# The last 96 columns of w1 ride with the third block of wqkv, and a table fixes the order of the work

## The chip, the cores and the metric

One Trainium2 chip, one core. The metric is the time of one execution on the device, in microseconds (us). TensorE is called PE, VectorE DVE, ScalarE ACT, GpSimd POOL; SyncE (SP) issues every DMA.

## The reference

The input x has 2048 tokens of 512 features. Two branches start from it and meet at the end:

```python
# A: attention, 32 heads of 16 features; each token sees itself and the
# 7 tokens at distances 2, 4, ..., 14 before it
qkv    = x @ wqkv                               # x has been normalised, 512 -> 3 x 512
logits = q . k[pos - 2*w] / 4     (w = 0..7)
o      = softmax(logits) . v[pos - 2*w]
a      = o @ wo
# B: channel mixing, hidden width F = 1376
b      = gelu(layernorm(...) @ w1 + b1) @ w2 + b2
out    = x + a * silu(b)
```

Both branches are fed with normalised rows of x, so that one transposed copy of the normalised tokens serves `x @ wqkv` and `x @ w1` alike.

## The kernel before, in words

**Accuracy.** Each fp32 factor of a product is split in two fp16 parts, a high and a low one, and a product is three matmuls: high by high, low by high, high by low. With a contraction over 512 = 4 x 128 features, that makes 12 matmuls for one output tile. Before a weight is split it is scaled by a power of two found from its sum of squares: ACT squares and accumulates (L421), PE adds up over the partitions (L435), DVE makes the factor (L439 to L459; `hsc` for w1 and the hidden layer, `zsc` for w2, `qsc` for wqkv). Then ACT writes the high part (L482 for w1 and w2, L536 for wqkv) and DVE the low part (L486, L543).

**Tokens.** The even and the odd tokens form two classes c, since all distances are even. A class has 8 token tiles of 128 tokens. `yT` holds their normalised and transposed high and low parts, in four tiles of 512 tokens.

**Attention.** It runs in 8 units, (class c, block hb of 128 features), hb = 0 to 3. In a unit, for each of 8 token tiles, 12 matmuls at L746 hold a piece of yT as the weights and stream 384 columns of `wq` (128 each of q, k and v) past it. ACT (L763) or DVE (L759) brings the 128x384 result into the tile `U`, of which there are two, used in turn. DMAs copy the rows that a token needs from other partitions (the halo, L771, with L776 and L777 for the corner by way of `misc`). DVE then makes the products of q and k (four of 128x2048 at L805), their sums (L808), the softmax (L822 to L837) and the products with v (four, L863); POOL and DVE add these up (L858, L873, L883). ACT and DVE split the result (L846, L848), and a DMA transposes it into `oT` (L851).

**MLP.** It runs in 4 chunks of 512 tokens by 11 blocks f of the hidden width; ten blocks have 128 columns, the last, f = 10, has FL = 96. `mlp1` (L1016) holds 128 (or 96) columns of w1 as the weights and streams 512 tokens of yT, 12 matmuls, into one of 3 PSUM banks `ps`. ACT applies gelu (L1033) and writes the high part (L1036), DVE the low part (L1038), which is the last reader of the bank; `h` has three buffers. `mlp2` (L1052) follows two blocks later: 4 token tiles by 3 matmuls of 512 columns, into 4 banks `z`. For f = 10 the hidden parts stand in a tile `hlast` of their own, whose row 96 holds a one that multiplies the bias b2, which stands as row 96 of w2's last block. The results of class 0 and 1 wait in DRAM (`gd`) until `wo` (L929 for class 0, L961 for class 1) closes the kernel, with a multiplication and an addition per tile on DVE (L993, L1000).

**Banks.** The L746 results use the same 3 banks `ps` and one more, `pl`.

**The order.** All work is first recorded as operations with engine, estimated cost, reads, writes and priority. `Plan.issue` then takes them one by one: at each step it looks at all operations whose inputs are there, takes the engine that can go earliest by its own cost estimates and, on that engine, the operation with the best priority; the DMAs on SP are ordered in the same way. So the program order on every engine comes out of estimates and not out of the text. Ring buffers (`R_ps`, `R_prod`, `R_f`, `R_h` and so on) are given out during this walk, the slot that came free first.

**At the start** the weights pass through buffers that later hold something else: w1's four pieces are loaded into `oT`, one `o` and one `h` buffer, w2 into the class 1 halves of yT and three `f` buffers, and the later blocks of wqkv follow into the same halves of yT when w2 has been split.

Of the kernel before, what the change touches and what calls it, by code (L numbers as in the profile page):

```python
# [18 lines left out]
P = 128  # L19
# [6 lines left out]
NHB = 4  # L26
# [12 lines left out]
LAG = 2  # L39

# [28 lines left out]
BEFORE_W1 = (0, 1, 4, 5)  # L69

# [26 lines left out]
class Plan:  # L97
# [89 lines left out]
    def place(self, o, t):  # L187

        if o.eng == "sp":
            if not o.nbytes:  # L190
                return t
            self.free["sp"] = t + o.issue
            self.dma = max(self.dma, t + o.issue + 0.3)
            self.dma += o.nbytes / (o.rate if self.dma > SLOW else 265e3)
# [12 lines left out]
        if o.port:  # L207
            self.portfree = end
        return end + LAT[o.eng]
# [12 lines left out]
    def issue(self):  # L222
# [104 lines left out]
def tile_mixer(ctx, tc, a_x, a_xt, a_wqkv, a_wo, b_w1, b_b1, b_w2, out):  # L327
# [34 lines left out]
    ident = sb.tile([P, P], F32, name="ident")  # L362
    make_identity(nc, ident)
    fours = sb.tile([P, 2 * P], BF16, name="fours")
    nc.vector.memset(fours, 4.0)
    mean1 = sb.tile([P, P], F32, name="mean1")
# [9 lines left out]
    wq = sb.tile([P, NHB, 2, KT, 384], F16, name="wq")  # L376
    w1 = sb.tile([P, 2, KT * F], F16, name="w1")
# [6 lines left out]
    b1T = sb.tile([P, NF], F32, name="b1T")  # L384
    hlast = sb.tile([P, 2, 512], F16, name="hlast")
# [81 lines left out]
    def low_pool(n, lo, get, s, hi, **k):  # L467
# [4 lines left out]
        pool(0.45 + n * 3.9e-3, fn, **k)  # L472
# [53 lines left out]
    def prep_q(hb):  # L526
# [3 lines left out]
        for k in range(0, KT, st):  # L530
            n = st * 384
            dst = [wq[:, hb, t, k:k + st].rearrange("p k e -> p (k e)") for t in range(2)]
            src = lambda k=k, n=n: stq[hb]()[:, k * 384:k * 384 + n]
# [117 lines left out]
    def y0(i):  # L651
# [12 lines left out]
        elif Y_ENG[i] == "pool":  # L664
            pool(1.25, lambda: nc.gpsimd.tensor_scalar(x(), x(), mv0[:, q, 0:1], rb0[:, q:q + 1], op0=ALU.subtract,
# [54 lines left out]

    def qkv(c, hb, u):
# [13 lines left out]
        raw = pl.users([("xc", j) for j in FP]) if u == 1 else set()  # L735
        csk = {i: (cs, g) for g in parts for i in g} if u == 0 else {i: cs for i in range(NI)}
        for n, i in enumerate((IORD0, IORD1)[u] if u < 2 else IORD):
# [5 lines left out]
            def mm(n0=0, n1=12, y=y, o=o, b=b):  # L743
                for n in range(n0, n1):
                    (s, t), k = ((0, 0), (1, 0), (0, 1))[n // KT], n % KT
                    nc.tensor.matmul(b.t[:, 0:384], y[:, s, k, o:o + P], wq[:, hb, t, k],  # L746
# [5 lines left out]
            for n0, n1 in zip([0] + ends, ends):  # L752
                pe(n1 - n0, 384, lambda mm=mm, n0=n0, n1=n1: mm(n0, n1), [("yh" if n1 <= 4 else "y", c, i)] +
# [8 lines left out]
            else:  # L762
                act(384, lambda i=i, b=b: nc.scalar.activation(  # L763
                    U3[:, i:i + 31:15, :], b.t[:, 0:384].rearrange("p (t e) -> p t e", t=3),
                    AF.Identity, scale=cs.t[:, cp(i):cp(i) + 1]), **ev)

# [241 lines left out]
    def mlp1(ch, f):  # L1008
        M = P if f < NF - 1 else FL
# [15 lines left out]
        if f < NF - 1:  # L1025
            h = R_h.new()
            hi, lo = (lambda: h.t[:, 0]), (lambda: h.t[:, 1])
        else:
            h = ("hlast",)
            hi, lo = (lambda: hlast[:, 0]), (lambda: hlast[:, 1])  # L1030
        hk = (h, 0) if f < NF - 1 else ("hlast", 0)
# [9 lines left out]
        hq[f] = (hi, lo, M if f < NF - 1 else M + 1, h, hk)  # L1041

    def mlp2(ch, f):
        hi, lo, K, h, hk = hq.pop(f)
        for t in range(4):
# [8 lines left out]
            pe(3, 512, mm, [h, hk, w2key[f]] + ([("hrow",)] if f == NF - 1 else []), [zt[t]])  # L1054
# [23 lines left out]
    def mlp(n):  # L1078
        for _ in range(n):
# [4 lines left out]
            if p < len(steps):  # L1084
                with prio(PR_M + p * 10):
                    mlp1(*steps[p])
# [18 lines left out]
    def zero_halo(b):  # L1105
# [7 lines left out]
          lambda: f32v(s1h.t, 1)[:, 0, 0:W1C[4] - W1C[3]]]  # L1113
# [4 lines left out]
    def load(kind, i, last=()):  # L1118
# [6 lines left out]
        elif kind == "w":  # L1125
            dma(P * 4 * (W1C[i + 1] - W1C[i]), lambda: nc.sync.dma_start(s1[i](), b_w1[:, W1C[i]:W1C[i + 1]]), [], s1k[i],
# [4 lines left out]
        elif kind == "b":  # L1131
            dma(P * 44, lambda: nc.sync.dma_start(b1T, b_b1), [], [("b1T",)], rate=20e3)
# [34 lines left out]
    for n in range(WAKE):  # L1167
        b = R_z[0].new()
        pl.add("pe", 0.2, lambda b=b: nc.tensor.matmul(b.t[:, 0:2 * P], fours[:, 0:P], fours, start=True,
# [11 lines left out]
    for n in range(4):  # L1181
        with prio(PS1):
            sumsq(lambda n=n: cw1.t[:, n:n + 1], (cw1, n), s1[n], s1k[n],
                  lambda n=n: w1f[0][:, W1C[n]:W1C[n + 1]], ("w1h", n), W1C[n + 1] - W1C[n])
# [9 lines left out]
    sumsq(lambda: col2.t[:, 0:1], (col2, 0), b1T, ("b1T",), lambda: junk, ("junk",))  # L1194
# [12 lines left out]
    for m, (f0, f1) in enumerate(W1P):  # L1207
        n = min(f0 // 4, 2) if f0 < 10 else 3
        c0, c1 = 512 * f0, min(512 * f1, KT * F)
        with prio(PW1 if m < W1FIRST else PR_H + 1 + (10 * f0 - 25) * 1e-6):  # L1210
            split(w1f[0][:, c0:c1], w1f[1][:, c0:c1], lambda n=n, c0=c0, c1=c1: s1[n]()[:, c0 - W1C[n]:c1 - W1C[n]], hsc[:, 0:1],
                  s1k[n] + [("hsc0",)] + [("w1h", j) for j in range(4) if W1C[j] < c1 and W1C[j + 1] > c0], ("w1", m),
                  W1ENG[m], n=c1 - c0, low=W1LO[m])
    pool(0.1, lambda: nc.gpsimd.memset(hlast[FL:FL + 1, 1], 0.0), [], [("hrow1",)])
    pool(0.6, lambda: nc.gpsimd.memset(hlast[FL:FL + 1, 0], 1.0), [], [("hrow0",)])
    pool(2.0, lambda: nc.gpsimd.tensor_scalar(hlast[FL:FL + 1, 0], hlast[FL:FL + 1, 0],
                                              hsc[FL:FL + 1, 2:3], None, op0=ALU.mult),
         [("hsc2",), ("hrow0",), ("hrow1",)], [("hrow",)])
# [148 lines left out]
```

## Time and profile before

| | |
|---|---|
| time, median of 3 runs | 414.59 us (414.57 to 415.31) |
| the profiled execution | 415.18 us |
| its span, first to last instruction | 413.4 us |
| granted TensorE clock in the span | 0.999 |
| PE, DVE, ACT, POOL busy | 98%, 92%, 54%, 29% |
| mean DMA traffic | 112 GB/s |

The difference between the execution's own time and its span, 1.8 us, lies around the instructions. Of the views used below, the groups of instructions give for each line the count, the total busy time in us and the mean ns of one, and behind the second bar the idle time before them with what ended it; the chain of waits gives the chain of work that ended last, in order of time, with the start, the length, the engine and the line of each step; a timeline gives the same for one engine, with consecutive instructions of one kind put together.

### The profile page before, as it was taken

The page shows a single profiled execution, that of the slowest core. Times are in us where ns is not written, and L with a number is a line of the kernel's source. Part 1 is how long each engine was busy: PE and PEld are TensorE (multiplying, and loading weights), DVE is VectorE, ACT ScalarE, POOL GpSimd, SP SyncE. Part 2 cuts the span into 40 slices and gives each one's busy share as a digit, 9 for nine tenths or more (in the row PEclk, how much of TensorE's full clock was granted, in tenths as well). Part 3 has the DMA queues.
Part 4 walks back from the last instruction along what each step waited for, and adds up shares of the span by engine and source line. Part 5 has one row for each costly group of instructions (what it writes and reads, how often), then busy time and mean ns, then how long its engine had stood idle before and what let it go on. Part 6 is the DMA issues. An engine that isn't in the chain of part 4 may idle for free.

```text
span 413.4 us, 5554 instructions
## 1 busy us (share of the span) xinstructions
PE 405.9 (98%) x2083; PEld 206.6 (50%) x2083; DVE 379.5 (92%) x379; ACT 222.1 (54%) x353; POOL 120.3 (29%) x131
## 2 busy tenths in 40 slices
PE   8799999999999999999999999999999999999996
PEld 5555544445654455445544554455455544444443
DVE  4996989998999999989998999999999998999954
ACT  4699899994549655843384252225212393263500
POOL 3834002004380425042504330434033404520021
PEclk9999999999999999999999999999999999999999
DMA  8958717030045137720172034223604244007133
GB/s 281 397 112 258 235 61 230 0 128 1 1 142 152 28 93 183 149 46 2 48 221 75 0 102 116 68 86 88 205 7 122 88 111 145 0 18 238 23 102 131
DMA packets 47211, 46.41 MB, mean 112 GB/s; under 512 B 31785, under 2 KB 32225, under 8 KB 46673
## 3 DMA queue, kind: packets, MB, share of 16 engines
q1 hardware_dynamic: 47184, 46.06, 37.6%
q8 instruction: 16, 0.26, 0.3%
q14 instruction: 11, 0.08, 0.1%
HBM read 24.06 MB, written 7.34 MB: 76 GB/s over the span
## 4 chain that ended last, share of the span: by engine, by line
PE 92%; ACT 3%; issue 1%; DVE 1%; POOL 1%; ACTq 0%
PE z L1052 28%; PE ps L1016 28%; PE ps L746 25%; PE ps L929 5%; PE ps L961 2%; PE z L961 2%; PE pl L746 1%; ACT w L421 1%; PE pl L961 1%; ACT f L673 1%; ACT yT L687 0%; ACT wq L536 0%; POOL wq L471 0%; POOL rb L635 0%; ACT prod L661 0%
## 5 line engine op out<-in xcount | busy, mean ns | idle before, releaser
L1016 PE MATMUL ps<-yT,w 128*128 128x512 f16 (+1 forms) x528 | 120.4, 379 | 0.0
L746 PE MATMUL ps<-wq,yT 128*128 128x384 f16 x708 | 117.0, 326 | 0.2 <-DVE U L759 0.2
L1052 PE MATMUL z<-w,h 128*128 128x512 f16 x480 | 110.4, 379 | 0.0
L746 PEld LDWEIGHTS <-yT 128*128 128x128 f16 x744 | 72.5, 98 | 49.2 <-issue 1.0
L1016 PEld LDWEIGHTS <-w 128*128 128x128 f16 (+1 forms) x528 | 52.8, 100 | 61.0
L805 DVE TENSOR_TENSOR prod<-U 128x2048 f32<-128x2048 f32 x32 | 73.2, 2286 | 2.2 <-POOL prod L883 0.7
L1052 PEld LDWEIGHTS <-h 128*128 128x128 f16 x480 | 46.6, 98 | 55.5 <-issue 0.3
L808 DVE TENSOR_REDUCE L<-prod 128x128 f32<-128x2048 f32 x32 | 73.0, 2281 | 0.4
L1033 ACT ACTIVATE ps<-ps,b1T,hsc 128x512 f32<-128x512 f32 (+1 forms) x44 | 32.9, 748 | 73.4 <-PE ps L1016 72.2
L863 DVE TENSOR_TENSOR prod<-pl,U 128x2048 f32<-128x2048 f32 x28 | 63.2, 2283 | 4.2 <-POOL prod L873 4.1
L763 ACT ACTIVATE U<-ps,cs 128x384 f32<-128x384 f32 x54 | 31.2, 580 | 65.2 <-PE ps L746 65.2
L873 POOL TENSOR_TENSOR prod<-prod,prod 128x2048 f32<-128x2048 f32 x7 | 31.7, 4531 | 113.8 <-DVE prod L863 99.6
L883 POOL TENSOR_TENSOR prod<-prod 128x1024 f32<-128x1024 f32 x14 | 32.9, 2349 | 0.0
L882 POOL COPY gate<-prod 1x1 f32<-1x1 f32 x21 | 5.5, 264 | 91.0 <-DVE prod L805 82.2
L1038 DVE SCALAR_TENSOR_TENSOR h<-ps,hsc,h 128x512 f16<-128x512 f32 x40 | 29.6, 741 | 1.7 <-ACT h L1036 1.4
L1036 ACT ACTIVATE h<-ps,hsc 128x512 f16<-128x512 f32 x40 | 27.3, 684 | 1.3 <-PE z L1052 0.4
L929 PE MATMUL ps<-wo,oT 128*128 128x512 f16 x96 | 21.7, 379 | 0.0
L858 DVE TENSOR_TENSOR prod<-prod,prod 128x2048 f32<-128x2048 f32 x9 | 20.5, 2282 | 0.0
L1033 ACT ACT_TABLE_LOAD x10 | 12.8, 1283 | 8.6 <-PE ps L1016 8.5
L883 POOL TENSOR_TENSOR prod<-prod,prod 128x1024 f32<-128x1024 f32 x7 | 16.4, 2347 | 0.0
L961 PEld LDWEIGHTS <-oT 128*128 128x128 f16 x108 | 10.6, 98 | 10.4
L929 PEld LDWEIGHTS <-oT 128*128 128x128 f16 x96 | 9.4, 98 | 11.2
(179 smaller groups left out, 377.8 us busy)
## 6 DMA issues: line engine op xcount, KB each, us to landing
f<-in_A_x_dram SPq DMA_DIRECT2D x31, 256.0 KB, 3.5
U<-U SPq DMA_DIRECT2D x16, 392.0 KB, 4.0
gd<-f SPq DMA_DIRECT2D x12, 256.0 KB, 3.4
prod<-in_A_x_dram SPq DMA_DIRECT2D x8, 256.0 KB, 6.9
oT<-in_B_w_dram SPq DMA_DIRECT2D x2, 1024.0 KB
yT<-in_B_w_dram SPq DMA_DIRECT2D x2, 1024.0 KB, 7.9
f<-gd SPq DMA_DIRECT2D x8, 256.0 KB, 2.7
out_dram<-f SPq DMA_DIRECT2D x8, 256.0 KB, 2.8
```

The source lines that it names most:

```text
L746: nc.tensor.matmul(b.t[:, 0:384], y[:, s, k, o:o + P], wq[:, hb, t, k], start=(n == 0), stop=(n == 11))
L763: act(384, lambda i=i, b=b: nc.scalar.activation(U3[:, i:i + 31:15, :], b.t[:, 0:384].rearrange("p (t e) -> p t e", t=3), AF.Identity, sca ...
L805: dve(2048, lambda p2=p2, g=g: nc.vector.tensor_tensor(p2(), q, slots(Ut, KH, 2 * g), op=ALU.mult), qk + [("kh", ub, 0), ("kh", ub, 1), (" ...
L808: dve(2048, lambda pr=pr, g=g: nc.vector.tensor_reduce(L3()[:, 2 * g:2 * g + 2], pr.t.rearrange("p (r f d) -> p r f d", r=2, d=DH), AX.X, ...
L863: dve(2048, lambda: nc.vector.tensor_tensor(pr.t.rearrange("p (r f d) -> p r f d", r=2, d=DH), A3()[:, 2 * g:2 * g + 2].rearrange("p r (f ...
L873: pool(4.75, lambda: nc.gpsimd.tensor_tensor(acc.t, acc.t, p1.t, op=ALU.add), [acc, p1], [acc])
L883: nc.gpsimd.tensor_tensor(x.t[:, 0:1024], x.t[:, 0:1024], y(), op=ALU.add)
L929: nc.tensor.matmul(b.t, oT[:, hb, i // 4, s, i % 4], wo[:, t, hb], start=(hb == 0 and n == 0), stop=(hb == last and n == 2))
L961: nc.tensor.matmul(b.t[:, cols], oT[:, hb, i // 4, s, i % 4], wo[:, t, hb, cols], start=(start and hb == 0 and n == 0), stop=(stop and hb ...
L1016: nc.tensor.matmul(b.t[0:M], w1[:, s, f * 512 + k * M:f * 512 + (k + 1) * M], yT[ch][:, t, k], start=(n == 0), stop=(n == 11))
L1033: act(512, lambda: nc.scalar.activation(b.t[0:M], b.t[0:M], AF.Gelu_apprx_tanh, bias=b1T[0:M, f:f + 1], scale=hsc[0:M, 1:2]), [b, ("b1T",) ...
L1052: nc.tensor.matmul(z.t, hl[s][0:K, t * P:(t + 1) * P], w2[0:K, w, f], start=(f == 0 and n == 0), stop=(f == NF - 1 and n == 2))
```

## The change

**The last 96 columns of w1** are put beside those of block hb = 2 of wqkv: the tile `wq2` is 480 columns wide, and `wl` names its last 96. In the two units with hb = 2 (u = 2 and u = 6) each L746 matmul (L848 in the changed kernel) streams 480 columns and not 384. The first 384 outputs go to `U` as before; ACT brings the other 96 into `hpt` (new, L870), with w1's scale in the same instruction. Here the hidden units lie along the columns and the tokens on the partitions, the other way round than in `mlp1`. So a new function `last_block`, called once per chunk, adds b1 as a row (POOL), applies gelu (ACT), writes the high (ACT) and the low part (DVE), each 128x384 for four token tiles, and a DMA transposes them into `hlt`, which `mlp2` reads for f = 10. The row of ones is set by POOL before the transpose. `mlp1` is no longer made for f = 10, and the three POOL instructions that prepared `hlast` are gone. b1 is loaded with a copy of its last 96 values in every partition, 54.8 KB in place of 5.5. The matmuls of hb = 2 now wait for the last piece of w1 as well.

**The order** no longer comes from the walk: a table ORDER of 1258 operation numbers gives it, and the slot of a ring is the one that came free first in that order. A few cost estimates are changed too, which have no say where the table rules. The constants ident and mean1 move into a tile `first`, which later serves as one of the `hpt`, and the 24 small matmuls without a use that keep PE occupied at the start (L1169, now L1279) read it; in the new order of PE 7 of these 24 stand behind the first L1125 (`mlp1`), where before all stood ahead of the first up-projection.

```diff
+HLAST = 2
+ORDER = (
+    0, 1, 2, 3, 4, 5, 6, 7, 8, 9, 10, 11, 19, 109, 117, 125, 114, 121, 130, 128, 108, 20, 123, 126, 129, 21, 33,
...
+)
@@ Plan.issue
-        order = []
+        order, fixed = [], [self.ops[n] for n in reversed(ORDER)]
...
+            if fixed:
+                o = fixed.pop()
+                t = max([self.earliest(o)] + [min(b.ring.free) for b in o.bufs if b.slot is None])
+                assert not o.npred and t < float("inf")
+                best = (t, o)
-            for e, cand in engs.items():
+            for e, cand in engs.items() if best is None else ():
...
-                    b.ring.free[b.slot] = b.end
+                    b.ring.free[b.slot] = len(order) if ORDER else b.end
@@ tiles
-    wq = sb.tile([P, NHB, 2, KT, 384], F16, name="wq")
-    w1 = sb.tile([P, 2, KT * F], F16, name="w1")
+    wq = [sb.tile([P, 2, KT, 384 + FL * (hb == HLAST)], F16, name=f"wq{hb}") for hb in range(NHB)]
+    w1 = sb.tile([P, 2, W1C[3]], F16, name="w1")
+    wl = wq[HLAST][:, :, :, 384:384 + FL]
...
-    hlast = sb.tile([P, 2, 512], F16, name="hlast")
+    hl0 = sb.tile([P, 512], F32, name="hl0")
+    hpt = [hl0[:, 0:512], first[:, 0:512]]
+    hlt = [h.bitcast(F16).rearrange("p (a t) -> p a t", a=2) for h in hpt]
@@ new
+    def last_block(ch):
+        n = 4 * FL
+        h16 = R_f.new()
...
+        def pads():
+            nc.gpsimd.memset(v()[:, :, :, FL:P], 0.0)
+            nc.gpsimd.tensor_scalar(v()[:, 0, :, FL], halves[:, 8:12], hsc[:, 2:3], 2.0, op0=ALU.mult, op1=ALU.mult)
...
+            pool(1.0, lambda: nc.gpsimd.tensor_tensor(x3(), x3(), row, op=ALU.add), xk + [("b1T",)], xk)
+            act(n, lambda: nc.scalar.activation(x, x, AF.Gelu_apprx_tanh), xk, xk,
+                aps=1, table="gelu")
+            act(n, lambda: nc.scalar.activation(v()[:, 0, :, 0:FL], x3(), AF.Identity, scale=hsc[:, 2:3]),
+                xk + [("hsc2",)], [(h16, 0)])
+            dve(n, lambda: nc.vector.scalar_tensor_tensor(v()[:, 1, :, 0:FL], x3(), hsc[:, 2:3], v()[:, 0, :, 0:FL],
+                                                          op0=ALU.mult, op1=ALU.subtract),
...
+            dma(P * 2048, lambda: nc.sync.dma_start_transpose(dst, h16.t.bitcast(F16)), [(h16, k) for k in range(3)],
@@ qkv
-                    nc.tensor.matmul(b.t[:, 0:384], y[:, s, k, o:o + P], wq[:, hb, t, k],
+                    nc.tensor.matmul(b.t[:, 0:wide], y[:, s, k, o:o + P], wq[hb][:, t, k],
...
+                   ([("w1", len(W1P) - 1)] if hb == HLAST else []) +
...
+            if hb == HLAST:
+                act(FL, lambda i=i, b=b: nc.scalar.activation(
+                    hpt[i // 4][:, (i % 4) * FL:(i % 4 + 1) * FL], b.t[:, 384:384 + FL], AF.Identity, scale=hsc[:, 1:2]),
+                    [b, ("hsc",)], [("hp", i // 4, i % 4)], prio=PEV, after=pl.users([("hp", i // 4, i % 4), ("hl", i // 4)]))
+        for j in range(2 if hb == HLAST else 0):
+            last_block(2 * c + j)
@@ mlp
-            if p < len(steps):
+            if p < len(steps) and steps[p][1] < NF - 1:
```

Three places of the new order matter below; in these rows a number behind a name tells buffers of one ring apart, and it is not the same in the two kernels.

**ACT, splitting w1** (`w_79` before, `w_81` after), from the factor `hsc` to the last high part of w1. Before, its rows stand thus, with two small rows on w2's last block and a table load between them:

```order
L482 ACTIVATE w_79<-oT,hsc 128x512
L482 ACTIVATE w_79<-oT,hsc 128x1024
L763 ACTIVATE U_87<-ps_140,cs_114 128x3x128
L482 ACTIVATE w_79<-oT,hsc 128x1024
L763 ACTIVATE U_86<-pl_142,cs_113 128x3x128
L1262 ACT_TABLE_LOAD
L1262 ACTIVATE warm<-halves 1x1
L482 ACTIVATE w_79<-oT,hsc 128x1024
L763 ACTIVATE U_87<-ps_139,cs_114 128x3x128
L1232 ACTIVATE w_80,s_121<-f_96 97x512
L482 ACTIVATE w_79<-o_105,hsc 128x1024
L482 ACTIVATE w_79<-h_106,hsc 128x384
```

After, L556 is what L482 was, L866 what L763 was; `f_103` and `f_104` are token tiles of class 1, whose mean and squares ACT takes for the normalisation (L773, L775, L777, before L699, L701, L703), and L495 squares the first half of w2. One more row, the high part of `o_107`, stands right ahead:

```order
L556 ACTIVATE wq_79<-h_108,hsc 128x4x96
L556 ACTIVATE w_81<-oT,hsc 128x1024
L556 ACTIVATE w_81<-oT,hsc 128x512
L866 ACTIVATE U_88<-pl_144,cs_115 128x3x128
L777 ACTIVATE f_103,mv_161<-f_103,mv_161 128x512
L866 ACTIVATE U_89<-ps_141,cs_116 128x3x128
L556 ACTIVATE w_81<-oT,hsc 128x1024
L773 ACTIVATE f_104,mv_161<-f_104 128x512
L775 ACTIVATE mv_161<-mv_161 128x1
L777 ACTIVATE f_104,mv_161<-f_104,mv_161 128x512
L495 ACTIVATE w_82,s_129<-yT_86 128x2048
L556 ACTIVATE w_81<-oT,hsc 128x1024
```

The two passes over token tiles and the squares of w2's half have moved ahead of w1's last high part; before, they come behind it.

**DVE, from w2's low parts to a low part of the hidden layer.** Before, the rows up to the fifth L1038 (`h_108`; four more stand ahead of these) are:

```order
L805 TENSOR_TENSOR prod_95<-U_86 128x2048
L1243 TENSOR_TENSOR zsc<-zsc,hsc 128x1
L486 SCALAR_TENSOR_TENSOR w_80<-yT_84,zsc,w_80 128x1024 x2
L486 SCALAR_TENSOR_TENSOR w_80<-yT_85,zsc,w_80 128x1024 x2
L486 SCALAR_TENSOR_TENSOR w_80<-f_97,zsc,w_80 128x512
L1038 SCALAR_TENSOR_TENSOR h_107<-ps_139,hsc,h_107 128x512
L808 TENSOR_REDUCE L_103<-prod_95 128x2x64
L1038 SCALAR_TENSOR_TENSOR h_108<-ps_140,hsc,h_108 128x512
```

After, the same line is L1143, the fifth of them is the last row here, L914 and L917 are the attention's products and sums (before L805 and L808), L937 and L938 the first two steps of the softmax:

```order
L560 SCALAR_TENSOR_TENSOR w_82<-yT_87,zsc,w_82 128x1024
L1143 SCALAR_TENSOR_TENSOR h_110<-ps_141,hsc,h_110 128x512
L560 SCALAR_TENSOR_TENSOR w_82<-yT_87,zsc,w_82 128x1024
L937 TENSOR_REDUCE mx_111<-L_105 128x64
L515 TENSOR_SCALAR ssq<-ps_141 128x1
L522 TENSOR_SCALAR s_127<-ssq 128x1
L528 TENSOR_SCALAR qsc<-s_127 128x1
L533 TENSOR_SCALAR qsc<-s_127 128x1
L938 TENSOR_TENSOR L_105<-L_105,mx_111 128x512
L560 SCALAR_TENSOR_TENSOR w_82<-f_102,zsc,w_82 128x512
L914 TENSOR_TENSOR prod_95<-U_89 128x2048
L1143 SCALAR_TENSOR_TENSOR h_109<-ps_142,hsc,h_109 128x512
```

From the first product to this fifth low part DVE's program now holds five L914 and four L917 where before it held three of each.

**SP, the halo of the first unit.** Before, both of its large copies (`U_86`, 112x896; one for k, one for v) stand ahead of w2's second half:

```order
L1129 DMA yT_85<-in_B_w_dram 128x2048
L771 DMA U_86<-U_86 112x896
L771 DMA U_86<-U_86 15x896
L771 DMA U_86<-U_86 112x896
L771 DMA U_86<-U_86 15x896
L776 DMA misc<-U_86 1x16x8
L1134 DMA f_97<-in_B_w_dram 128x512
L1134 DMA f_98<-in_B_w_dram 128x512
L1129 DMA yT_84<-in_B_w_dram 128x2048
```

After, L880 is what L771 was, the first unit's tile is `U_88`, and its first copy stands eight rows further up; the rows shown lead up to its second:

```order
L579 DMA yT_86<-in_A_wqkv_dram 128x768 x2
L880 DMA U_88<-U_88 15x896
L880 DMA U_89<-U_89 15x896 x2
L880 DMA U_89<-U_89 112x896
L885 DMA misc<-U_88 1x16x8
L880 DMA U_89<-U_89 112x896
L885 DMA misc<-U_89 1x16x8
L1025 DMA f_103<-in_A_x_dram 128x512
L579 DMA yT_87<-in_A_wqkv_dram 128x768
L1025 DMA f_104<-in_A_x_dram 128x512
L880 DMA U_88<-U_88 112x896
```

The second copy has moved behind the loads of wqkv's third block into yT_86 and of part of its fourth into yT_87, buffers that w2's two halves occupy until DVE has written their low parts.

More of the change, by code (lines that the diff above doesn't have):

```diff
@@ L360, in tile_mixer @@
     PR_H, PR_U, PR_M = 200.0, 1000.0, 1000000.0
-    ident = sb.tile([P, P], F32, name="ident")
+    first = sb.tile([P, 512], F32, name="first")
+    ident, mean1 = first[:, 0:P], first[:, P:2 * P]
     make_identity(nc, ident)
-    fours = sb.tile([P, 2 * P], BF16, name="fours")
+    fours = sb.tile([P, P], BF16, name="fours")
     nc.vector.memset(fours, 4.0)
-    mean1 = sb.tile([P, P], F32, name="mean1")
     nc.vector.memset(mean1, 1.0 / D)
@@ L1024, in mlp1 @@
                after=pl.users([b]))
[L1025 to L1031, printed above, removed]
+        h = R_h.new()
+        hi, lo = (lambda: h.t[:, 0]), (lambda: h.t[:, 1])
+        hk = (h, 0)
         with prio(PR_H + pl.prio * 1e-6):
@@ L1168, in tile_mixer @@
         b = R_z[0].new()
-        pl.add("pe", 0.2, lambda b=b: nc.tensor.matmul(b.t[:, 0:2 * P], fours[:, 0:P], fours, start=True,
+        pl.add("pe", 0.2, lambda b=b: nc.tensor.matmul(b.t[:, 0:2 * P], fours, mean1.bitcast(BF16), start=True,
                                                        stop=True), [], [b], prio=1e9)
@@ L1210, in tile_mixer @@
         with prio(PW1 if m < W1FIRST else PR_H + 1 + (10 * f0 - 25) * 1e-6):
[L1211 removed]
+            dst = [w1f[t][:, c0:c1] if n < 3 else wl[:, t] for t in range(2)]
+            split(*dst, lambda n=n, c0=c0, c1=c1: s1[n]()[:, c0 - W1C[n]:c1 - W1C[n]] if n < 3 else s1[n](), hsc[:, 0:1],
                   s1k[n] + [("hsc0",)] + [("w1h", j) for j in range(4) if W1C[j] < c1 and W1C[j + 1] > c0], ("w1", m),
                   W1ENG[m], n=c1 - c0, low=W1LO[m])
[L1214 to L1218, printed above, removed]
     pl.prio = PU1
```

53 lines of the change are left out of this document (35 added, 18 removed), and 60 rows, old and new, of the table ORDER.

## The prediction

> **What bounds the kernel now.** I read the busy shares first, then what PE waits for, then the chain of waits.
>
> ```profile
> PE 405.9 (98%) x2083; PEld 206.6 (50%) x2083; DVE 379.5 (92%) x379; ACT 222.1 (54%) x353; POOL 120.3 (29%) x131
> ```
> ```profile
> PE z L683 <- POOL prod L665: 1.6, 1, 1.6
> PE z L1169 <- DVE fours L365: 1.2, 1, 1.2
> PE z L683 <- DVE prod L668: 0.4, 1, 0.4
> PE ps L746 <- DVE U L759: 0.2, 1, 0.2
> ```
> ```profile
> 31.39 0.67 PE pl L746 x4
> ...
> 56.74 0.01 PE z L435
> ...
> 101.60 15.60 PE ps L746 x96
> ...
> 119.14 2.59 PE ps L1016 x12
> ...
> 408.45 1.32 PE ps L961 x12
> ...
> 409.80 0.49 DVE U L993
> ```
>
> PE is busy 98% of the span. All its waits (columns: total, times, longest) come to 3.4 us and belong to the filling of the kernel. In the chain (start, length, step) PE follows upon PE from 31.39 to 409.77 us; then comes a tail of 3.6 us to the span's end at 413.4. So a matmul that goes shortens the kernel by its pitch, **as long as no other engine takes over the end**, and DVE with 92% is the candidate.
>
> The pitch is read from the same rows: 2.59/12 = 0.216 us with 512 columns, 15.60/96 = 0.1625 with 384. Between them lie 0.0534 us per 128 columns. As a check I count what the order puts behind the step at 56.74: 1188 matmuls of 512 columns, 576 of 384, 24 of 256 (at half of 0.216). That is 256.5 + 93.6 + 2.6 = 352.7 us, ending at 409.4; the trace has 409.77, so 0.3 us falls to small steps.
>
> **The change part by part. First, PE.** It loses `mlp1` for f = 10: 4 chunks x 12 = 48 matmuls of 512 columns, though with only 96 columns of weights:
>
> ```profile
> L1016 PE MATMUL ps<-yT,w 128*96 128x512 f16 x48 | 11.0, 379 | 0.0
> L1033 ACT ACTIVATE ps<-ps,b1T,hsc 96x512 f32<-96x512 f32 x4 | 3.0, 743 | 17.2 <-PE ps L1016 17.2
> L1036 ACT ACTIVATE hlast<-ps,hsc 96x512 f16<-96x512 f32 x4 | 2.7, 680 | 0.1
> L1038 DVE SCALAR_TENSOR_TENSOR hlast<-ps,hsc,hlast 96x512 f16<-96x512 f32 x4 | 3.0, 744 | 1.9 <-ACT hlast L1036 1.9
> ```
>
> 48 x 0.216 = 10.4 us go. Two units x 8 token tiles x 12 = 192 matmuls grow from 384 to 480 columns. No row shows 480; by the line between the two pitches each costs 0.040 more, 7.7 in all. The bounds are 0 (the pitch of 384) and 0.0534 (that of 512), so 0 to 10.3; I take 7.7, since both neighbours lie on one line through about zero. **Balance: -2.7 us.**
>
> The Trainium skill ("TensorE: Matmul & The Clock Gate", section "Back-to-back issue gap") gives a sustained spacing of about 131 ns at 512 columns and 81 at 128, and 2.5 ns plus 1/2.4 ns per column for an isolated matmul. The 0.216 and 0.1625 of this trace agree with the isolated rule and not with the sustained one. By the sustained one, 48 x 0.131 = 6.3 would go and 192 x 0.0125 = 2.4 come, an estimate of -3.9.
>
> PE also gets something. 7 of the 24 matmuls without a use, all early before, now stand among the work behind the first up-projection:
>
> ```profile
> L1169 PE MATMUL z<-fours x24: 272/421/421, 1.2 to 10.9; 128*128 128x256 bf16 x24
> ```
>
> The shortest of them lasts 272 ns against 379 for one of 512 columns, so the pitch is 0.107 shorter, 0.109. Seven cost 0.8 us where PE has no idle time, and nothing where it waits anyway. With them the balance is -1.9.
>
> **ACT, DVE and POOL.** ACT loses 4 x (0.743 + 0.680) = 5.7 us, DVE 4 x 0.744 = 3.0. ACT gains 16 evictions of 128x96; no row has that shape.
>
> ```profile
> L763 ACT ACTIVATE U<-ps,cs 128x384 f32<-128x384 f32 x54 | 31.2, 580 | 65.2 <-PE ps L746 65.2
> L883 POOL TENSOR_TENSOR prod<-prod 128x1024 f32<-128x1024 f32 x14 | 32.9, 2349 | 0.0
> ```
>
> They lie between the 0.19 of a 128x1 (below, at 45.60) and the 0.58 of the 128x384 here, 3.0 to 9.3 in all; by the line between, 0.29 each, 4.6. Gelu and high part of 4 chunks at 128x384 add 8 x 0.6 = 4.8, DVE's low parts 4 x about 0.6 = 2.4. ACT so ends 3.7 us up, with 46% idle; DVE 0.6 us down. POOL's 4 additions of 128x384 and their pads cost at most 2.35 each per instruction, by the row of 128x1024. All this hides beside PE: the first `hpt` is wanted by `mlp2` f = 10, not sooner than the unit's own 8 tiles of 12 x 0.2 us and further steps. If that cover went, one chunk's chain (addition, gelu, high, low and a transpose) would be in the open.
>
> **The start of the attention.** Here I expect most of the gain to be lost. The first product on DVE stands behind the last low part of w1 in both orders, and that waits for ACT's last high part. ACT's rows of before:
>
> ```profile
> 32.58 1.75 ACT L482 ACTIVATE w<-oT,hsc 128x512 f16<-128x512 f32 x2
> ...
> 34.69 1.14 ACT L482 ACTIVATE w<-oT,hsc 128x1024 f16<-128x1024 f32 x1
> ...
> 40.88 0.60 ACT L482 ACTIVATE w<-h,hsc 128x384 f16<-128x384 f32 x1
> ...
> 41.85 0.61 ACT L699 ACTIVATE f<-f 128x512 f32<-128x512 f32 x1
> ...
> 42.46 1.89 ACT L421 ACTIVATE w<-yT 128x2048 bf16<-128x2048 f32 x1
> ...
> 45.60 0.19 ACT L701 ACTIVATE mv<-mv 128x1 f32<-128x1 f32 x1
> ...
> 46.31 0.71 ACT L703 ACTIVATE f<-f,mv 128x512 f32<-128x512 f32 x1
> ```
>
> Each begins about 0.1 before the one ahead ends, so I count 1.04 for a 128x1024, 0.50 for 128x384, 0.83 for 128x512, 0.46 for an eviction. Before, the last high part ended at 40.88 + 0.60 = 41.5. In the new order stand, from the first high part: 1.04 + 0.50 + 1.04 + 0.83, eviction 0.46, square pass 0.70, eviction 0.46, 1.04, the second token tile's 0.61 + 0.10 + 0.70, w2's squares 1.89, and 1.13 for the last: 10.5 us. The first started at 32.58; part of a token tile's pass (0.61) stands ahead of it now, so I take 32.9 of 32.6 to 33.3. The last high part then ends at 43.4.
>
> ```profile
> 42.27 1.28 DVE L486 SCALAR_TENSOR_TENSOR w<-o,hsc,w 128x1024 f16<-128x1024 f32 x1
> ...
> 43.99 2.28 DVE L805 TENSOR_TENSOR prod<-U 128x2048 f32<-128x2048 f32 x1
> ...
> 57.03 0.15 DVE L439 TENSOR_REDUCE s<-z 128x1 f32<-128x5 f32 x1
> ...
> 57.72 2.28 DVE L805 TENSOR_TENSOR prod<-U 128x2048 f32<-128x2048 f32 x1
> ...
> 59.99 4.87 DVE L486 SCALAR_TENSOR_TENSOR w<-yT,zsc,w 128x1024 f16<-128x1024 f32 x4
> 64.77 0.75 DVE L486 SCALAR_TENSOR_TENSOR w<-f,zsc,w 128x512 f16<-128x512 f32 x1
> 65.43 0.75 DVE L1038 SCALAR_TENSOR_TENSOR h<-ps,hsc,h 128x512 f16<-128x512 f32 x1
> 66.09 2.28 DVE L808 TENSOR_REDUCE L<-prod 128x128 f32<-128x2048 f32 x1
> 68.29 0.74 DVE L1038 SCALAR_TENSOR_TENSOR h<-ps,hsc,h 128x512 f16<-128x512 f32 x1
> ...
> 78.03 0.68 DVE L828 TENSOR_REDUCE mx<-L 128x64 f32<-128x512 f32 x1
> ```
> ```profile
> L1038 DVE SCALAR_TENSOR_TENSOR h<-ps,hsc,h 128x512 f16<-128x512 f32 x40 | 29.6, 741 | 1.7 <-ACT h L1036 1.4
> ```
>
> The last low part takes about 1.2 more, a handover 0.1: **first product at 44.7** and not 43.99. From there to the end of the fifth L1038 the old order needed 69.03 - 43.99 = 25.0 us (three products and three sums). The new one holds five and four, at 2.20 each (66.09 to 68.29) 19.8; w2's low parts 4.78 (59.99 to 64.77) and 0.66; five hidden low parts at 0.66, 3.3; two softmax steps 1.2; the factors for w2 0.69 (57.03 to 57.72) and for wqkv four steps like the one at 57.03, about 0.5; a small clearing 0.1: 31.0. Gaps of some 0.5 come on top, and waits for ACT's `h`, of which the whole kernel of before has 1.4, here 0 to 1.2; I take 0.3. **The fifth low part ends at 44.7 + 31.8 = 76.5.**
>
> The next matmul that needs its PSUM bank is an up-projection. From it to the end the order has 1056 matmuls of 512 columns, 384 of 384, 192 of 480, 24 of 256: 228.0 + 62.4 + 38.9 + 2.6 = 331.9, with the 0.3 of the check 332.2 us. Without any wait PE would end at 409.8 - 2.7 = 407.1, so it would stand there at 74.9, with the seven idle matmuls at 75.7. DVE frees the bank at 76.5: PE waits 0.8 us, in all 1.6 of the 2.7 us are gone, and PE ends at 408.7, **-1.1 us**. The profiled run took 415.18, so 414.1 for it; the median lies 0.6 lower, so **413.5 us**.
>
> **SP.** The first unit's second halo copy now stands behind loads of wqkv that wait for w2's low parts:
>
> ```profile
> U<-U SPq DMA_DIRECT2D x16, 392.0 KB, 4.0
> f<-in_A_x_dram SPq DMA_DIRECT2D x31, 256.0 KB, 3.5
> yT<-in_A_wqkv_dram SPq DMA_DIRECT2D x4, 384.0 KB, 4.0
> ```
>
> The last of these low parts stands three DVE rows before the factors for wqkv: 44.7 + 8 x 2.20 + 4 x 0.66 + 0.69 + 4.78 and gaps, 71.2. SP then has three issues, so the copy starts at about 72.5 and lands at 76.5. The first product with v needs it at 76.5 + 3.0 = 79.5 (one more low part, three softmax steps, one low part of wqkv). It is hidden by 3 us if the transfers overlap.
>
> **The rivals.**
> A, the forecast: DVE holds one up-projection back by about 0.8 us. With the first product between 44.2 and 45.5: 412.8 to 414.5.
> B, no wait: the first product starts by 43.9 (ACT finds part of its passes done while it waits for `hsc`, where the old trace has 0.7 us of idle time). Then the balance of -1.9 shows: 412.7. Against it, 10.5 us of ACT work stand between.
> C, the gain is eaten: the high parts begin at 33.3 and the 1.2 us of waits for `h` return in full. Low part at 77.8, PE ends at 410.0: 414.8.
> D, slower: the three transfers run one after the other. Then the load issued at 71.2 lands at 75.2, the token tile at 78.7, the halo at 82.7, 3.2 us after it is wanted; DVE, on which PE already waits, passes that on: 416.7. It decides from 79.5 on. For it: SP's queue is in order. Against it: 256 KB take 3.5 and 392 KB 4.0, so most of a landing is a fixed time that can overlap.
> E, wider matmuls cost far less than columns say, as if the weight loads set the pitch: 192 x 0.0125 in place of 7.7, with what goes shrinking to 6.3: -3.9 + 0.8, 411.5. The two pitches of the trace speak against it.
>
> **How the numbers follow.** Chances: A 0.45, B 0.21, C 0.15, D 0.17, E 0.02. The measurement tells about 0.2% (0.83 us) from no change, so faster means below 413.76. Of A some six tenths lie there, with B and E 0.50; same 0.30 (the rest of A, most of C); slower 0.20 (D and the edge of C). The range runs from 412.1 (below B) to 416.7 (the middle of D), leaving out some 0.15.
>
> **What would show it.** PE's groups: 192 fewer pitches of 384, a chain step with 480 columns at 0.2025 per matmul, no `128*96` rows. ACT's timeline: the last high part of w1 ends near 43.4. DVE's timeline: first product near 44.7, fifth hidden low part ending near 76.5. PE's waits: one of about 0.8 us on L1125 for DVE `h` L1143 near 76, and none after. A wait of DVE's L972 for a DMA into `U` near 80 is D; waits of PE on `hpt`'s path (L1161 for the transpose) would be a thing I have not priced and make me wrong, as would a late chain of waits that ends on DVE.

## The result: slower by 1.35%

The changed kernel takes 420.12 us (median of 4 runs, 419.58 to 421.56), the kernel before 414.58 beside it (414.49 to 415.31). The ratio is 1.0135 with a 95% interval from 1.0108 to 1.0163. The forecast was 413.5 with a range up to 416.7. The profiled execution took 420.24 us, its span 418.5, which is 5.1 us more span than before.

The busy shares of the changed kernel, and what its PE waits for (in total, times, longest):

```profile
PE 404.2 (97%) x2035; PEld 200.9 (48%) x2035; DVE 386.4 (92%) x379; ACT 223.7 (53%) x370; POOL 129.3 (31%) x140
```
```profile
PE ps L682 <- DVE f L676: 1.6, 1, 1.6
PE z L1279 <- DVE first L438: 1.2, 1, 1.2
PE ps L1125 <- DVE ssq L515: 1.0, 1, 1.0
PE z L691 <- DVE U L684: 0.8, 1, 0.8
PE ps L848 <- DVE s L515: 0.7, 1, 0.7
```

PE has 1.7 us less to do (by its busy time), but two waits behind the start are new, 1.7 us together, and both are for a tiny DVE step (L515, 128x1). The chain of waits (start, length, step) has the wide matmuls and the end:

```profile
287.41 2.43 PE ps L848 x12
...
408.60 1.32 PE ps L1070 x12
409.92 0.03 issue
409.94 0.49 DVE U L1102
```

Twelve matmuls of 480 columns take 2.43 us, 0.2025 each. PE ends at 409.92, where it ended at 409.77 before: **PE has gained nothing, and the loss lies behind it**. From PE's end to the span's end there are 8.6 us in place of 3.6. The last stretches by engine (start and end, length, then PE, PEld, DVE, ACT and POOL busy with counts, PE's clock, DMA share, GB/s), first of the changed kernel, then of the one before:

```profile
405.00:410.00 5.00, 4.91 (x31) 2.74 (x28) 3.90 (x7) 0.00 (x0) 0.86 (x1) 1.00 0.00 0
410.00:415.00 5.00, 0.00 (x0) 0.00 (x0) 1.19 (x3) 0.00 (x0) 0.40 (x1) 0.70 0.64 230
415.00:419.00 4.00, 0.00 (x0) 0.00 (x0) 0.00 (x0) 0.00 (x0) 0.00 (x0) 0.50 0.46 172
```
```profile
405.00:410.00 5.00, 4.76 (x34) 3.14 (x32) 3.49 (x7) 0.00 (x0) 0.00 (x0) 1.00 0.37 138
410.00:414.00 4.00, 0.00 (x0) 0.00 (x0) 0.71 (x2) 0.00 (x0) 0.00 (x0) 0.82 0.25 86
```

Now the transfers stand still from 405 to 410 us and 1.8 MB follow (230 GB/s x 5 us + 172 x 4), as much as seven of the 256 KB tiles; before, the tiles left one by one as they were ready. SP's program says why. The last rows of it, after:

```order
L960 DMA_TRANSPOSE oT<-o_107 128x8x128
L1092 DMA f_98<-in_A_x_dram 128x512
L1111 DMA out_dram<-U_88 128x512
L1111 DMA out_dram<-U_88 128x256
L1111 DMA out_dram<-U_88 128x512 x2
L1111 DMA out_dram<-U_88 128x256
L1111 DMA out_dram<-U_88 128x512 x4
```

The second of the nine output transfers is a 128x256 tile, and DVE writes the two of that size last of all; seven transfers stand behind it, and SP issues them in the order of its program. What SP waits for at these transfers (in total, times, longest), after and before:

```profile
SPq L1111 <- DVE U L1109: 9.9, 1, 9.9
```
```profile
SPq L1002 <- DVE U L1000: 5.2, 5, 2.2
```

One wait of 9.9 us for DVE stands where five short ones were. Before, the seven full tiles stand first and the two halves last.

The other new thing is at 84 us. DVE's and POOL's timelines of the changed kernel:

```profile
83.99 0.74 DVE L1143 SCALAR_TENSOR_TENSOR h<-ps,hsc,h 128x512 f16<-128x512 f32 x1
84.65 4.04 DVE L1349 TENSOR_TENSOR zsc<-zsc,hsc 128x1 f32<-128x1 f32 x1
88.61 2.27 DVE L917 TENSOR_REDUCE L<-prod 128x128 f32<-128x2048 f32 x1
90.81 0.14 DVE L515 TENSOR_SCALAR ssq<-ps 128x1 f32<-128x1 f32 x1
```
```profile
84.15 4.52 POOL L982 TENSOR_TENSOR prod<-prod,prod 128x2048 f32<-128x2048 f32 x1 [17.47 <-DVE prod L972]
```

A product of 128x1 lasts 4.04 us and ends when POOL's addition ends (84.15 + 4.52 = 88.67). The same step took 0.15 before. What PE waits for at 91.0 stands two rows behind it.

### The profile page after: what moved, and what is told of

It reads as the page before. It is cut to its first block, busy times and chain, and to the rows that moved or that the text cites. A ratio compares the mean times of both kernels' runs of the same rounds, so it can differ in the third digit from the quotient of the medians.

```text
span 418.5 us, 5475 instructions
## 1 busy us (share of the span) xinstructions
PE 404.2 (97%) x2035; PEld 200.9 (48%) x2035; DVE 386.4 (92%) x379; ACT 223.7 (53%) x370; POOL 129.3 (31%) x140
## 4 chain that ended last, share of the span: by engine, by line
PE 77%; DVE 15%; issue 4%; ACT 1%; DMA 1%; POOL 0%; DVEq 0%; ACTq 0%
PE ps L848 25%; PE z L1161 22%; PE ps L1125 18%; PE ps L1038 5%; PE ps L1070 2%; PE z L1070 2%; DVE L L917 2%; DVE w L560 2%; DVE prod L914 2%; DVE prod L972 2%; DVE h L1143 1%; PE pl L691 1%; DVE zsc L1349 1%; PE pl L848 1%; DVE wq L617 1%
## 5 line engine op out<-in xcount | busy, mean ns | idle before, releaser
L848 PE MATMUL ps<-wq,yT 128*128 128x384 f16 (+1 forms) x708 | 130.2, 337 | 0.9 <-DVE s L515 0.7
L1161 PE MATMUL z<-w,h 128*128 128x512 f16 x480 | 113.5, 379 | 0.0
L1125 PE MATMUL ps<-yT,w 128*128 128x512 f16 x480 | 110.4, 379 | 1.0 <-DVE ssq L515 1.0
L848 PEld LDWEIGHTS <-yT 128*128 128x128 f16 x744 | 72.5, 98 | 60.3 <-issue 1.8
L914 DVE TENSOR_TENSOR prod<-U 128x2048 f32<-128x2048 f32 x32 | 75.2, 2348 | 1.4
L1125 PEld LDWEIGHTS <-w 128*128 128x128 f16 x480 | 46.8, 98 | 56.2 <-issue 1.2
L917 DVE TENSOR_REDUCE L<-prod 128x128 f32<-128x2048 f32 x32 | 73.0, 2283 | 0.6
L982 POOL TENSOR_TENSOR prod<-prod,prod 128x2048 f32<-128x2048 f32 x7 | 34.2, 4881 | 72.5 <-DVE prod L972 61.5
L1138 ACT ACTIVATE ps<-ps,b1T,hsc 128x512 f32<-128x512 f32 x40 | 29.7, 747 | 49.1 <-PE ps L1125 48.9
L866 ACT ACTIVATE U<-ps,cs 128x384 f32<-128x384 f32 x54 | 30.9, 576 | 38.4 <-PE ps L848 38.4
L1143 DVE SCALAR_TENSOR_TENSOR h<-ps,hsc,h 128x512 f16<-128x512 f32 x40 | 29.4, 743 | 3.5 <-ACT h L1141 3.5
L1038 PE MATMUL ps<-wo,oT 128*128 128x512 f16 x96 | 21.9, 379 | 0.0
L955 ACT ACTIVATE o<-prod,osc 128x1024 f16<-128x1024 f32 (+1 forms) x9 | 9.4, 1049 | 15.6 <-DVE prod L967 10.3
L1070 PEld LDWEIGHTS <-oT 128*128 128x128 f16 x108 | 10.6, 98 | 10.4
```

What stands on the lines that cost most here:

```text
L848: nc.tensor.matmul(b.t[:, 0:wide], y[:, s, k, o:o + P], wq[hb][:, t, k], start=(n == 0), stop=(n == 11))
L866: act(384, lambda i=i, b=b: nc.scalar.activation(U3[:, i:i + 31:15, :], b.t[:, 0:384].rearrange("p (t e) -> p t e", t=3), AF.Identity, sca ...
L914: dve(2048, lambda p2=p2, g=g: nc.vector.tensor_tensor(p2(), q, slots(Ut, KH, 2 * g), op=ALU.mult), qk + [("kh", ub, 0), ("kh", ub, 1), (" ...
L917: dve(2048, lambda pr=pr, g=g: nc.vector.tensor_reduce(L3()[:, 2 * g:2 * g + 2], pr.t.rearrange("p (r f d) -> p r f d", r=2, d=DH), AX.X, ...
L982: pool(4.75, lambda: nc.gpsimd.tensor_tensor(acc.t, acc.t, p1.t, op=ALU.add), [acc, p1], [acc])
L1038: nc.tensor.matmul(b.t, oT[:, hb, i // 4, s, i % 4], wo[:, t, hb], start=(hb == 0 and n == 0), stop=(hb == last and n == 2))
```

## The experiments

Three theories. **T1**: the order of the output transfers alone makes the end late. **T2**: a DVE step that reads two SBUF tensors stands still while POOL adds two, and the 4 us so lost hold PE up between 84 and 100 us. **T3**: the matmuls without a use that now stand among the work cost PE their pitch. The rivals stand in the expectations. Times are medians beside runs of the kernel before on the same chip (414.85 to 414.92). In the kernels with a `moved` call (below) the line numbers of the trace are some ten larger.

**Output order in the changed kernel (e1_out)**

```diff
+def moved(order, ns, after):
+    rest = [n for n in order if n not in ns]
+    k = rest.index(after) + 1
+    return tuple(rest[:k]) + tuple(ns) + tuple(rest[k:])
+ORDER = moved(ORDER, (1218, 1233, 1223, 1243, 1248, 1238, 1257, 1253), 1228)
```

> The changed kernel with its nine output transfers in the order in which their tiles become ready, the two 128x256 ones last. Theory: in the changed kernel the second transfer in SP's program is a 128x256 tile that DVE writes last, and seven others stand behind it; the order alone makes the end late. Then the stretch from PE's last matmul to the span's end shrinks from 8.6 us to about 3.6, PE's end stays at 409.9, and the time falls from 420.1 to 415.2. Rival: the transfers themselves are slow there (about 380 GB/s whoever comes first), and the order is harmless; then it stays at 420.

Measured 416.77 (416.16 to 416.86), 1.0039 of before, interval 1.0024 to 1.0054. PE's last matmul ends at 410.5 there and the span at 415.0, so the end takes 4.5 us, not 8.6. T1 holds for 4.1 of the 5.0 us of longer end; 0.9 stay. PE's end, which I expected to stay at 409.9, came 0.6 later.

**The same order in the kernel before (e3_before_out)**

```diff
+        tail = [x for x in order if x[1].eng == "sp"][-9:]
+        order = [x for x in order if x not in tail] + [tail[k] for k in (0, 7, 5, 2, 8, 4, 1, 6, 3)]
         for t, o in order:
             o.fn()
```

> The kernel before, with nothing changed but the order of its nine output transfers, put as in the changed kernel (512, 256, 512, 512, 256, then four of 512 columns). Theory (the order alone costs the tail): the stretch behind PE's last matmul grows from 3.6 to about 8.5 us, 414.6 becomes 419.5. Rival (the tail belongs to something else in the changed kernel): within 0.5 us of 414.6.

Measured 418.27 (418.13 to 418.53), 1.0079 (1.0064 to 1.0094): 3.35 us slower through nothing but the order of nine transfers. SP's wait and the stretch behind PE (columns as above) look like those of the changed kernel:

```profile
SPq L1004 <- DVE U L1002: 9.5, 1, 9.5
```
```profile
410.00:415.00 5.00, 0.00 (x0) 0.00 (x0) 0.42 (x1) 0.00 (x0) 0.00 (x0) 0.67 0.99 362
```

The stretch behind PE grows to 7.0 us and not to 8.5, so the size is smaller than the 4.9 expected. The rate is not the reason: once they flow, the transfers run at about 340 to 390 GB/s in both kernels. The 128x256 tile for which all wait is complete earlier here, at 409.19 us, 0.3 ahead of PE's end; in the changed kernel DVE completes it at about 410.9, 1.0 behind PE's end.

**Two small DVE steps moved (e2_port), on top of e1_out**

```diff
+ORDER = moved(ORDER, (245,), 277)   # the zsc step L1349, ahead of the second L972
+ORDER = moved(ORDER, (278,), 398)   # the four steps on qsc, behind the third L972
```

> As e1_out, and two small DVE steps moved: the 128x1 product of zsc and hsc that lasted 4.04 us goes ahead of the second product with v, and the four small steps on qsc behind the third one, so that neither stands beside POOL's addition of 128x2048. Theory: such a DVE step with its operands in SBUF does not run while POOL's addition does; moved, it lasts about 0.15 us, PE's waits of 0.96 us (L1125) and 0.71 us (the first 480-column matmul) go, PE ends near 408.2 and the time is 413.5. Rival: the two waits come from the chain of sums and would only move; then as e1_out, 415.2, with the small step short or not.

Measured 414.48 (413.63 to 414.95, 10 runs), 0.9987 (0.9977 to 0.9996). The step takes 0.15 us and PE has no wait left behind the start. The time falls by 2.3 us. In e1_out's trace PE's waits behind the start came to 1.9 us, 1.5 of it for the small DVE steps; what makes the rest is not shown.

**Only the zsc step moved (e2a_zsc)**: the first of these two lines alone.

> As e1_out, with only the 128x1 product of zsc and hsc moved ahead of the second product with v; the four small steps on qsc stay, and now come up while POOL's addition of 128x2048 (4.5 us) still runs. Theory (a DVE step with operands in SBUF only stands until POOL's addition ends): the zsc step lasts 0.15 us, but the second of the four steps on qsc, the first that reads SBUF alone, lasts about 1.5 us and ends when the addition ends; DVE gains 2 to 2.5 us of the 4, PE's wait of 0.96 us goes and the one of 0.71 goes or nearly; time 414.5 to 415. Rival (the one step was slow for a reason of its own): the qsc steps last 0.15 each, DVE gains 4.

Measured 414.02 (413.18 to 415.39, 10 runs), 0.9987 (0.9974 to 0.9999). Here the expectation missed. DVE's and POOL's timelines:

```profile
84.21 2.27 DVE L927 TENSOR_REDUCE L<-prod 128x128 f32<-128x2048 f32 x1
86.40 0.15 DVE L525 TENSOR_SCALAR ssq<-ps 128x1 f32<-128x1 f32 x1
86.58 0.15 DVE L532 TENSOR_SCALAR s<-ssq 128x1 int32<-128x1 int32 x1
86.77 0.15 DVE L538 TENSOR_SCALAR qsc<-s 128x1 int32<-128x1 int32 x1
```
```profile
83.71 4.55 POOL L992 TENSOR_TENSOR prod<-prod,prod 128x2048 f32<-128x2048 f32 x1 [17.55 <-DVE prod L982]
```

Steps that read one SBUF tensor (86.58, 86.77) take their 0.15 us in the middle of POOL's addition (83.71 to 88.26). So T2 is narrower than I had put it there: it is not any step with its operands in SBUF.

**Another form in the same place (e10_form), on top of e1_out**

```diff
-    dve(1, lambda: nc.vector.tensor_tensor(zsc[:, 1:2], zsc[:, 1:2], hsc[:, 3:4], op=ALU.mult),
+    dve(1, lambda: nc.vector.tensor_scalar(zsc[:, 1:2], zsc[:, 1:2], hsc[:, 3:4], None, op0=ALU.mult),
```

> As e1_out, the zsc step in its old place beside POOL's addition, but written as a product of a tile with a scalar per partition and no longer as a product of two tiles. Theory (only a DVE step that reads two SBUF tensors stands still during POOL's addition of two): it lasts about 0.2 us, DVE gains nearly 4 us, PE's waits of 0.76 and 0.70 us go, time 414 to 414.5. Rival (the place or the data matter, not the form): 4 us again, 416.8.

```profile
85.42 0.20 DVE L1358 TENSOR_SCALAR zsc<-zsc,hsc 128x1 f32<-128x1 f32 x1
```

0.20 us, at the old place beside POOL's addition, where the two-input form takes 4.04 in e1_out too; PE's two waits are gone; 414.83 (413.42 to 416.07, 10 runs), 0.9995 (0.9980 to 1.0009). The form decides, neither the place nor the data.

**The step in the kernel before, put beside POOL's addition (e7_before_port)**

```diff
+        z = next(x for x in order if x[1].n == 248)
+        order.remove(z)
+        order.insert(1 + next(k for k, x in enumerate(order) if x[1].n == 530), z)
```

> The kernel before, with the 128x1 product of zsc and hsc (0.15 us there) moved so that it comes up at about 95.8 us, while POOL's addition of 128x2048 (93.1 to 97.7) runs. Theory: the step lasts until that addition ends, about 1.8 us in place of 0.15; DVE waited 1.89 us there for ACT, so the time stays at 414.9. Rival (the 4.04 us belong to something in the changed kernel): 0.15 us.

```profile
95.85 1.86 DVE L1246 TENSOR_TENSOR zsc<-zsc,hsc 128x1 f32<-128x1 f32 x1
```
```profile
93.16 4.54 POOL L876 TENSOR_TENSOR prod<-prod,prod 128x2048 f32<-128x2048 f32 x1 [24.55 <-DVE prod L866]
```

1.86 us, ending at 97.71 with POOL's addition (97.70), in a kernel that has nothing of the change. The time is 414.98 (0.9987 to 1.0012 of before), since DVE had to wait for ACT there anyway.

**Matmuls without a use left out (e4_wake, e8_wake)**

```diff
-        pl.add("pe", 0.2, lambda b=b: nc.tensor.matmul(
+        pl.add("pe", 0.2, lambda b=b, n=n: n >= 13 or nc.tensor.matmul(                               (e4_wake)
+        pl.add("pe", 0.2, lambda b=b, n=n: n in (2, 3, 5, 8, 10, 12, 14, 16, 19, 23) or nc.tensor.matmul(   (e8_wake)
```

> As e2_port, and 11 of the 24 matmuls without a use are left out, those that the table puts among the work behind the first of wqkv (they compute nothing that is read). Theory: each costs PE 0.109 us where PE has no idle time, 0.8 for the seven behind the first up-projection, up to 1.2 for all; with no wait of PE left in e2_port the time falls by that, 414.5 to 413.5. Rival: PE's end is set elsewhere (DVE's or a transfer's readiness) and new waits take the place; then 414.5.

Measured 414.88 (0.9990 to 1.0008). The choice by number was wrong: six of those behind the first wqkv matmuls were still there, and mostly early ones were gone. So this run says next to nothing on T3.

> As e2a_zsc, and this time the ten matmuls without a use that stand behind the first ones of wqkv (three at 24 to 30 us, seven behind the first up-projection) are left out; e4_wake had left out 11 others, mostly at the start. Theory: seven or more cost PE 0.109 us each, PE waits for nothing there, so PE's end and the time fall by 0.8 to 1.1 us, 414.0 to about 413.1. Rival: DVE, not PE, then sets the pace between 75 and 100 us, PE gets new waits of the same sum, and the time stays at 414.

Measured 414.52 (413.53 to 416.24, 12 runs), 0.9987 (0.9973 to 1.0001), no gain over e2a_zsc. PE has new waits, which were not there with these matmuls:

```profile
PE z L519 <- ACT w L1348: 0.4, 1, 0.4
PE ps L1135 <- ACT U L876: 0.3, 1, 0.3
PE ps L858 <- ACT U L876: 0.3, 1, 0.3
PE ps L858 <- DVE yT L774: 0.2, 1, 0.2
```

1.2 us of waits stand for ten times 0.109, and from the first matmul of wqkv to PE's end the two profiles have the same 393.1 us. So T3 is not borne out: the matmuls filled time in which PE would have waited, mostly for ACT, up to the sums of w2 at 52 us.

**The last tiles in another order (e6_best on e4_wake, e9_best on e8_wake)**: PE's and DVE's last steps and the outputs are moved within the table, in e9_best by these lines (1206, 1235: the tile that POOL completes).

```diff
+ORDER = moved(ORDER, (1206,), 1230)
+ORDER = moved(ORDER, (1235, 1240, 1208, 1245, 1250, 1254), 1216)
+ORDER = moved(ORDER, (1231, 1232, 1222, 1217, 1236, 1237, 1241, 1242, 1246, 1247, 1251, 1252, 1255, 1256), 1254)
+ORDER = moved(ORDER, (1218, 1233, 1223, 1238, 1243, 1248, 1253, 1257), 1228)
```

> As e4_wake, and the last eight output tiles of PE in another order: the tile whose addition POOL makes (1.26 us) is no longer the last full one, the additions of the two half tiles follow each its own multiplication. Theory: the stretch from PE's end to the span's end, 4.5 us in e1_out and e2_port, goes back to 3.6 as in the kernel before; 0.8 us less than e4_wake, 412.7, below both kernels. Rival: the output transfers (1.8 MB in the last 11 us) set the end and the order of the tiles changes nothing.

Measured 415.87 (1.0015 to 1.0034), a loss: DVE's last multiplications and additions came in a heap behind PE.

> As e8_wake, and among the last eight output tiles the one with POOL's addition comes before the last full one, with a full tile of twelve matmuls between two multiplications of DVE (e6_best had put two multiplications and three additions of DVE in a heap at the end). Theory: the stretch from PE's last matmul to the span's end shrinks from 4.5 us to 3.6 to 4, time 0.5 to 0.9 below e8_wake, near 412.5. Rival: the last transfers, each of 128 to 256 KB behind one another, set the end whatever the order of the tiles; no difference to e8_wake.

Measured 414.16 (413.75 to 414.77, 12 runs), 0.9980 of before (0.9970 to 0.9989). It is the furthest below the kernel before, by 0.2%; the intervals of e2_port and e2a_zsc lie below 1 too, and overlap with this one. But the end did not shrink as expected: from PE's last matmul (406.25 + 1.47) to the span's end (412.3) there are 4.6 us, against 4.5 in e2a_zsc, so what it owes to this order, and what to the noise of e8_wake, is not shown.

**The wide block without the table (e5_walk)**

```diff
-ORDER = (0, 1, 2, ..., 1218,)
+ORDER = ()
```

> The changed kernel with the table empty, so that the walk by cost estimates orders it as it did before: the 480-column block without the table. Theory (the wide block is worth 2.7 us on PE and the table gives it away): 412 to 413, with PE's matmuls of 480 columns at 0.2025 us. Rival (the wide block itself brings waits, through the wait for w1's last piece or the chain of the last block): 414.6 or more, with new waits of PE in the units that hold the wide block.

Measured 426.13 (425.19 to 427.58), 1.0271 (1.0243 to 1.0299). The longest of PE's waits there:

```profile
PE ps L1063 <- DVE h L1081: 3.7, 1, 3.7
PE z L1099 <- ACT w L494: 2.1, 1, 2.1
PE z L1099 <- DVE w L498: 1.7, 1, 1.7
```

The time is on the rival's side, but its mechanism is not seen: no wait of PE is at the 480-column matmuls. The 3.7 stands at 139 us in the up-projection, the 2.1 and 1.7 at 65 and 67 us for w2's split. This walk, whose estimates and priorities are partly changed too, put w2's split and the hidden low parts late. So the table is not what loses time against this walk; it is 6 us better, with two faults in it. What the wide block is worth in the order of the kernel before, no run shows.

## Why the prediction was wrong, point by point

**The step that failed** is "then comes a tail of 3.6 us to the span's end". I carried it over as a constant and worked out only where PE ends. It measured 8.6. The forecast for the profiled execution was 414.1 and its time 420.24; 5.0 of these 6.1 us are the tail, and 1.2 are PE's end, 409.92 and not 408.7. The tail is made by SP's program, which the new table orders too; I followed SP's order at one place, the halo copy, and not at its last nine rows. Put back, the order gives 420.12 to 416.77 (against before +5.5 to +1.9 us), and put into the kernel before, it costs 3.35.

**The second fault** cost 1.9 to 2.8 us: 416.77 in e1_out against 414.83, 414.48 and 414.02 in the three kernels whose zsc step does not stand still. The prediction gave PE one wait near 76 us "and none after". My DVE sum ended at the fifth hidden low part; the zsc step, which the kernel before has ahead of w2's low parts, comes later in the new order, and I put it at nothing. In the trace of before it took 0.15 with POOL idle at 59.9 us; in the new order it comes up at 84.65, half a microsecond behind the start of POOL's addition. The Trainium skill ("SBUF — State Buffer", section "SBUF: two separate sides") says that a DVE instruction with two SBUF inputs and a GpSimd instruction that reads SBUF shut each other out for a whole instruction. The 4.04 us, the 1.86 in e7_before_port and the 0.20 of the one-input form agree with it. A table fixes the order on each engine, but not the moment at which the steps of two engines meet.

I overlooked that the trace of before already had such a step:

```profile
34.86 0.89 DVE L1198 SCALAR_TENSOR_TENSOR s<-s,s 128x1 f32<-128x1 f32 x1
```
```profile
34.42 1.33 POOL L470 TENSOR_SCALAR oT<-oT,hsc 128x1024 f32<-128x1024 f32 x1 [6.56 <-ACT w L482]
```

It reads two SBUF tensors, ends with POOL's step at 35.75, and takes 0.16 in the changed kernel, where POOL is idle. POOL's step there reads one tensor and a scalar, so the hold does not need an addition of two.

**PE's balance** was right in kind and size: 0.2025 for 480 columns where 0.2025 was worked out, and the balance of -2.7 with it; with the seven matmuls without a use -1.9 was worked out, and PE's busy time fell by 1.7. By the sustained spacing of the Trainium skill ("TensorE: Matmul & The Clock Gate", section "Back-to-back issue gap") a gain of 3.9 was the estimate; the 2.43 us for twelve speak against it.

**The matmuls without a use** were sized at 0.8 us and cost nothing that e8_wake could find, since waits of 1.2 us took their place.

**The first product** was put at 44.7 and began at 42.28; the fifth hidden low part was put at 76.5, and it and the sixth were done by 75.2. ACT's last high part of w1, put at 43.4, ended at 44.7. The chain from it to DVE's first product does not exist: the low part of that last piece is made by POOL (44.80 to 48.12), and DVE's last low part of w1 began at 41.09. I had taken "the last low part" to be DVE's. PE had no wait at that place, so the loss that I forecast (0.8 us) was none, and rival B was nearest to the truth up to 84 us.

**The halo (rival D)** did no harm: SP issued the copy at 70.29 where I had 72.5, and the first product with v began at 77.99 without a wait for a DMA.

**ACT's evictions** of 128x96 took 0.34 each, between my line (0.29) and the upper bound (0.58), and were hidden as forecast.

**What is left.** The kernels with both faults mended stand 0 to 0.2% below the kernel before, and not the 2.7 us of the balance. Their end is 0.9 us longer (4.5 against 3.6); where this comes from stays open, and two attempts (e6_best, e9_best) did not shorten it. PE's end, 407.7 in e2a_zsc against 409.8, has 2.1 of the 2.7, but single profiles differ in the start: in the nine of the table's order the first matmul of wqkv began between 14.64 and 15.94 us, in the three of the kernel before's own order between 15.53 and 16.05, and all that follows shifts with it. From that matmul to PE's end there are 393.8 to 393.9 us in these three and 392.5 to 393.1 in the seven of the table's order without the 4 us step, 0.7 to 1.4 less. The ten matmuls without a use in that stretch, or the waits in their place, take 1.1 of the 2.7; the rest, 0.2 to 0.9, stays open.

## What to carry to other kernels

When an order is rewritten, read every engine's queue to its last row, above all the one that carries the output: a transfer whose data come last, put second, holds up all that is ready, and no view of the kernel before shows that. A sum of durations on one engine is only good while the other engine's steps stay where they were; two-input DVE steps need to be looked for beside POOL's, and a duration in the old trace that does not fit a step's shape, as the 0.89 above, is a hint of it. And a step that looks last in a chain should be followed to the engine that really makes it.

## What the runs showed of the hardware that was not expected

A DVE step of 128x1 with two SBUF inputs lasted 4.04 us beside an addition of POOL that has as much, and 0.15 with POOL idle; with one SBUF input and a scalar per partition 0.20 beside the same addition, and products with v, one input of which lies in PSUM, did not wait for it either (in e2a_zsc the first of two began at 86.90, beside the addition, and the two took 4.48 us). It goes the other way too: POOL's additions of 128x2048 (L982) take 4.52 us at the least, but the one that began at 129.74 took 5.42, beside a DVE step with two SBUF inputs (L560) that had begun at 129.49 and ended at 130.76. Also a large product can be caught: of the 32 products of q and k (L914), one lasted 3.33 us where the median is 2.29, beside POOL's subtraction on w1, which ended at 48.12.

```profile
46.94 3.33 DVE L914 TENSOR_TENSOR prod<-U 128x2048 f32<-128x2048 f32 x1
```
```profile
46.00 2.12 POOL L545 TENSOR_TENSOR w<-oT,w 128x1024 f16<-128x1024 f32 x1
```
